# The first fold of the attention products: from a VectorE sum to an adding DMA of GpSimd

## The chip, the cores and the metric

The kernel runs on one core of a Trainium2 chip. The core has five engines with instruction queues of their own: TensorE (PE in the profile, with its weight loads as PEld), VectorE (DVE), ScalarE (ACT), GpSimd (POOL) and SyncE (SP). Data moves by 16 DMA engines; an engine's queue issues a transfer, and its end is told by a semaphore. The metric is the device time in microseconds (us) of one execution, taken as the median of several runs.

## What is computed

Two branches read the same layer-normalised input `xn` (2048 tokens, 512 features), and their outputs are added to `x`.

```
x  = A_x;  xn = layernorm(x)
q, k, v = split(xn @ wqkv)                 # 32 heads of 16
logits[s, w] = q[s] . k[s - 2 w] / 4       # w = 0..7, a dilated window of 8 keys
o[s] = sum_w softmax(logits)[s, w] v[s - 2 w]
A  = o @ wo
z  = gelu(xn @ w_in);  z1, z2 = halves of z (688 each);  z2 = layernorm(z2)
g  = w_sp @ z2 + b_sp                      # mixes over the 2048 tokens
B  = (z1 * g) @ w_out
out = x + A + B
```

The change lies in the logits of branch A.

## The kernel before, in words

The order of work on each of the five queues is written out by hand in five lists of names (`pe`, `act`, `dve`, `pool`, `sp`); a name stands for a few instructions, and `needs` says which names must be done first. A queue runs its list strictly in order: where one name waits, all names behind it on that queue wait as well.

TensorE goes through these stages: the z2 half of `w_in` (names z), the q and k heads (L350), the v heads (L350), the z1 half (names y, L247), the mixing over tokens (names M0 to M15, L512, 32 matmuls each), and the output products (L566, L573, L580). All of z, heads, y and M write to three PSUM buffers in turn: a stage step may start when ScalarE has emptied the buffer three steps back (M0 needs the emptying of y13, named yg13).

The attention logits are made without TensorE. q and k lie with 4 token groups of 32 heads on the 128 partitions. The 16 features of a head are dealt with in four chunks c = 0..3, and the tokens in two halves th = 0, 1, so there are eight units (c, th). A unit has three steps:

- `m{c}{th}` (products, L393): two VectorE multiplications of 128x4096 elements, one for each pair of features; where (c, th) is in `EARLY` the second is cut into two.
- `f{c}{th}` (fold, L398 or L401): the second 128x4096 array is added to the first. For seven units GpSimd issues two adding DMAs of 512 KB each (L401); for unit (0, 0) VectorE does one sum (L398).
- `p{c}{th}` (logits, L406 to L409): VectorE adds the two remaining features and the sum over chunks, in `a_sb`.

The units use four pairs of buffers. (0, 0), (1, 1) and (3, 0) share the first one, so m11 needs p00. The products of chunk c need k with its halo, the 16 keys that a token group takes from its neighbour. They are copied by small DMAs: `kh0a`, `kh0b` and `kh1` on SyncE's queue, `kh2` and `kh3` on GpSimd's (L368, L369). kh1 is made of 8 runs of 32 bytes per partition on 96 partitions and 4 on 32.

On VectorE stand between these steps the statistics of z2: zs8, zs12 (L307 to L310) and zb8, zb12 (L318), with zr8, zr12 (L314) on GpSimd between the two. After zb12 ScalarE normalises z2 tiles 12 to 15 (zn12 to zn15, L330), in turn with yg12 to yg15 (L339).

SyncE's queue at the time of the first units holds: kh0a, kh0b, W0, kh1, wv, W1, vh. W0 and W1 are transposing loads of 256 rows of `w_sp` (L489), wv loads the 512 KB of v weights (L258), vh copies v's halo. M0 needs W0, M2 needs W1.

GpSimd's queue at that time holds: zr4, kh2, f01, f10, zr8, f11, kh3, f20 and so on. kh2 waits for ScalarE's k casts of chunk 2 (L363).

Of the kernel before, what the change touches and what calls it, by code (L numbers as in the profile page):

```python
# [10 lines left out]
ALU = mybir.AluOpType  # L11
# [5 lines left out]
NT = S // P  # L17
# [25 lines left out]
def kernel(  # L43
# [13 lines left out]
    V = nc.vector  # L57
# [26 lines left out]
    b16 = sb.tile([NT, P], BF16, name="b16")  # L84
# [40 lines left out]
    ph = [[prod[n][:, a * PU // 2:(a + 1) * PU // 2] for a in range(2)] for n in range(2)]  # L125
# [268 lines left out]

    def fold(c, th):
        x = PU // 4
        if (c, th) == (0, 0):
            V.tensor_tensor(ph[0][0], ph[0][0], ph[0][1], ALU.add)  # L398
            return
        for n in range(2):  # L400
            G.dma_start(*[h[:, n * x:(n + 1) * x] for h in ph[BUF[c, th]]], accum_op=ALU.add)  # L401

# [8 lines left out]
    for c, th in BUF:  # L411
        n = f"{c}{th}"
        b = BUF[c, th]
        over = {2: ALLN + ALLX, 3: [f"p{1}{0}"] + [f"{a}{p}" for a in "qk" for p in range(8)]}.get(b, [])
        op_(f"m{n}", over + [f"qc{2 * c}", f"qc{2 * c + 1}"] + (["kh0a", "kh0b"] if c == 0 else [f"kh{c}"]) + ([last[b]] if b in last else []),
            lambda c=c, th=th: products(c, th))
        op_(f"f{n}", [f"m{n}"], lambda c=c, th=th: fold(c, th))
        op_(f"p{n}", [f"f{n}"], lambda c=c, th=th: logits(c, th))
        last[b] = f"p{n}"
# [249 lines left out]
    for i in range(6, NT):  # L669
        dve += [f"ag{i + 1}"] * (i + 1 < NT) + [f"b{i + 2}"] * (i + 2 < NT) + [f"n{i}"]  # L670
    dve += """zt0 zt1 zt2 zt3 zt4 zt5 zn0 zn1 zn2 zn3 zt6 zt7 zn4 zn5 zn6 zn7
        m00 f00 p00 m01 zs8 m10 m11 p01 zb8 m20 p10 m21 p11 zs12 m30 p20 zb12 m31 p21 p30 X0 HW p31 u0 X1 C0 g0 a0.0 u1 a0.1 C1 g1 g2
        a0.2 g3 a0.3 g4 a0.4 g5 a0.5 a0.6 g6 a0.7 g7 a0.8 a0.9 g8 a0.10 a0.11 g9 g10 a1.0 a1.1 g11 a1.2 g12 a1.3
        a1.4 g13 a1.5 g14 a1.6 a1.7 g15 a1.8 a1.9 a1.10 a1.11 a1.12 a1.13""".split()
    OUT = [i for n in range(3) for i in groups[n]] + tail
    dve += [f"F{i}" for i in OUT[:12]] + ["Fe"] + [f"F{i}" for i in OUT[12:]] + ["Fl0", "Fl1", "Fl2"]
    pool = ["b16"] + [f"gr{i}" for i in range(NT)] + "zr0 zr4 kh2 f01 f10 zr8 f11 kh3 f20 f21 zr12 f30 f31 LO5 V00 V01 V02 V03".split()
    sp = """x0 x1 x2 wz0 wz1 wz2 x3 x4 x6 wy x8 x12 wk t4 t5 t6 t7 t8 t9 t10 t11 t12 t13 t14 t15 wq kh0a kh0b W0 kh1 wv W1 vh
        W2 W3 LO0 LO1 W4 U0 W5 LO2 LO3 U1 U2 W6 LO4 U3 U4 W7 U5 U6 U7 U8 U9 U10 R0 U11 U12 U13 V10 V11 R1 U14 V12 U15 V13""".split()
    sp += [f"S{i}" for i in OUT] + ["Sl0", "Sl2"]  # L680
# [53 lines left out]
```

## Time and profile before

| | us |
|---|---|
| median of 3 runs | 200.03 (199.96 to 200.37) |
| profiled execution, whole time | 199.44 |
| its span, first to last instruction | 197.7 |
| TensorE busy | 192.8 (98% of the span) |
| VectorE busy | 179.2 (91%) |
| ScalarE busy | 87.9 (44%) |
| GpSimd busy | 43.4 (22%) |

The granted TensorE clock was 1.000. In the views shown below a row of a timeline gives the start in us, the duration in us, the engine, the line of the kernel, the operation, the output and input names, the shapes, the count of instructions merged into the row, and in brackets the idle time ahead of it with what ended it. A row of the DMA queues gives packets, megabytes, and the time that the packets took as a share of all 16 engines in that window: q0 holds what GpSimd issues, q1 what SyncE issues. This share can pass 100%, since a packet that is stalled counts for as long as it is open.

### The profile page before, as it was taken

How to read it: one execution, taken by the hardware profiler on the slowest of the kernel's cores; microseconds unless marked ns; L12 is line 12 of the kernel's file. 1: busy time of each engine (PE TensorE's matmuls, PEld its weight loads, DVE VectorE, ACT ScalarE, POOL GpSimd, SP SyncE). 2: the span in 40 equal slices, each digit the busy share in tenths (PEclk: the TensorE clock that was granted, in tenths of full speed). 3: DMA queues.
4: the chain of work that ended last, by engine and by line, in shares of the span. 5: the costliest groups of instructions: out<-in, count | busy, mean ns of one | idle time of the engine just before them, and what ended most of it. 6: DMA issues, size and time to landing. Idle time of an engine off the chain costs nothing.

```text
span 197.7 us, 4588 instructions
## 1 busy us (share of the span) xinstructions
PE 192.8 (98%) x1944; PEld 121.5 (61%) x1944; DVE 179.2 (91%) x214; ACT 87.9 (44%) x128; POOL 43.4 (22%) x79
## 2 busy tenths in 40 slices
PE   7899999999999999999999999999999999999993
PEld 2466666666666666666666666666666654444442
DVE  4899896799989999999999999999999999999073
ACT  2476798785558967792562311112221110044000
POOL 4477322001565326355000000011120000000000
PEclk9999999999999999999999999999999999999999
DMA  4999552499999999989699999999979227402433
GB/s 148 354 338 133 90 107 83 71 154 135 254 206 211 202 185 146 190 177 185 128 209 252 186 217 276 162 242 266 213 154 241 54 48 219 86 2 83 136 106 106
DMA packets 71252, 33.40 MB, mean 169 GB/s; under 512 B 59488, under 2 KB 69248, under 8 KB 71104
## 3 DMA queue, kind: packets, MB, share of 16 engines
q1 hardware_dynamic: 68400, 25.38, 61.6%
q0 software_dynamic: 2688, 7.70, 20.0%
q8 instruction: 15, 0.25, 0.5%
q10 hardware_dynamic: 144, 0.03, 0.1%
q14 instruction: 5, 0.04, 0.1%
HBM read 10.13 MB, written 2.10 MB: 62 GB/s over the span
## 4 chain that ended last, share of the span: by engine, by line
PE 93%; DMA 2%; SPq 1%; DVE 1%; issue 1%; DVEq 0%
PE mm L512 38%; PE mm L350 21%; PE mm L247 18%; PE mm L580 7%; PE mm L566 6%; PE aux L566 2%; DMA z<-in_A_x_dram 2%; PE mm L573 1%; SPq L255 1%; SPq L165 1%; PE aux L225 0%; DVE stats L172 0%; DVE z L628 0%; DVE z L186 0%; PE aux L580 0%
## 5 line engine op out<-in xcount | busy, mean ns | idle before, releaser
L512 PE MATMUL mm<-z,wsp 128*128 128x344 bf16 x512 | 74.8, 309 | 0.0
L512 PEld LDWEIGHTS <-wsp 128*128 128x128 bf16 x512 | 50.1, 98 | 24.6
L350 PE MATMUL mm<-xnT,wts 128*32 128x512 bf16 x768 | 41.7, 379 | 0.0
L247 PE MATMUL mm<-wts,xnT 128*128 128x344 bf16 x256 | 38.3, 309 | 0.0
L350 PEld LDWEIGHTS <-wts 128*32 128x32 bf16 x768 | 28.7, 139 | 12.8 <-issue 0.3
L460 DVE TENSOR_TENSOR prod<-vp,a_sb 128x4096 bf16<-128x4096 bf16 x16 | 36.2, 2282 | 0.0
L247 PEld LDWEIGHTS <-xnT 128*128 128x128 bf16 x256 | 24.6, 98 | 12.5 <-ACT xnT L228 0.6
L528 ACT ACTIVATE qk<-mm,b_col 128x688 bf16<-128x688 f32 x16 | 13.3, 830 | 42.4 <-PE mm L512 40.2
L393 DVE TENSOR_TENSOR prod<-qk 128x4096 bf16<-128x4096 bf16 (+1 forms) x15 | 27.2, 1860 | 1.2 <-ACT qk L363 1.1
L464 DVE TENSOR_TENSOR prod<-prod,prod 128x8192 bf16<-128x8192 bf16 (+1 forms) x7 | 26.7, 3809 | 0.1
L363 ACT CAST qk<-mm 128x1024 bf16<-128x1024 f32 x16 | 16.2, 1012 | 8.2 <-PE mm L350 8.2
L580 PE MATMUL mm<-wts,xnT 32*128 32x512 bf16 x192 | 14.5, 374 | 0.0
L523 POOL DMA_DIRECT2D qk<-qk x8 | 3.9, 497 | 47.9 <-DMA qk<-z 40.3
L339 ACT ACTIVATE z<-mm 128x688 bf16<-128x688 f32 x16 | 11.8, 742 | 4.2 <-PE mm L247 3.4
L264 ACT ACTIVATE z<-mm 128x688 bf16<-128x688 f32 x16 | 11.8, 744 | 3.2 <-PE mm L247 3.2
L566 PEld LDWEIGHTS <-qk 128*128 128x128 bf16 x75 | 7.3, 98 | 8.9 <-issue 0.4
L566 PE MATMUL mm<-wts,qk 128*128 128x512 bf16 x55 | 12.4, 379 | 0.0
L172 DVE BATCH_NORM_STATS2 stats<-z 128x6 f32<-128x512 bf16 x15 | 10.1, 673 | 2.0 <-DMA z<-in_A_x_dram 1.9
L401 POOL DMA_DIRECT2D prod<-prod x10 | 8.8, 978 | 11.6 <-DVE prod L393 11.6
L580 PEld LDWEIGHTS <-xnT 32*128 32x128 bf16 x256 | 6.7, 93 | 7.2
L183 POOL TENSOR_TENSOR rstd<-rstd,mhalf 128x1 f32<-128x1 f32 x16 | 9.0, 562 | 3.7 <-DVE rstd L200 2.6
L616 ACT CAST z<-mm 128x512 bf16<-128x512 f32 x6 | 3.3, 600 | 13.6 <-PE mm L580 13.6
(93 smaller groups left out, 179.0 us busy)
## 6 DMA issues: line engine op xcount, KB each, us to landing
prod<-prod POOLq DMA_DIRECT2D x10, 512.0 KB, 7.9
wts<-in_A_wo_dram SPq DMA_DIRECT2D x4, 512.0 KB, 6.7
wsp<-in_A_x_dram SPq DMA_DIRECT2D x2, 1024.0 KB, 6.5
out_dram<-z SPq DMA_DIRECT2D x15, 128.0 KB, 1.8
wts<-in_A_wqkv_dram SPq DMA_DIRECT2D x3, 512.0 KB, 6.4
z<-in_A_x_dram SPq DMA_DIRECT2D x2, 512.0 KB, 7.6
wsp<-z POOLq DMA_DIRECT2D x2, 512.0 KB, 8.8
wsp<-wts POOLq DMA_DIRECT2D x2, 512.0 KB, 8.4
```

Of the source, the lines that this page charges most:

```text
L247: PE.matmul(t[:, hh, 0:FHALF], xnT[:, kc, i * P:(i + 1) * P], w_z[part][:, kc, hh * FHALF:(hh + 1) * FHALF], start=(kc == 0), stop=(kc == ...
L264: A.activation(z2[:, i, :].rearrange("p (a b) -> p a b", a=2), t[:, :, 0:FHALF], ACT.Gelu_apprx_tanh, **total)
L339: op_(f"yg{i}", [f"y{i}"] + ["p10"] * (i >= 10), lambda: A.activation(z1u[:, i, 0:FH].rearrange("p (a b) -> p a b", a=2), t[:, :, 0:FHALF] ...
L350: PE.matmul(t[32 * g:32 * g + 32, dd, :], w, r, start=(kc == 0), stop=(kc == C - 1), tile_position=(0, 32 * g))
L363: op_(f"{a}c{p}", [f"{a}{p}"], lambda: A.copy(home(a, p), t[:].rearrange("p d (t s) -> p d t s", t=2)))
L393: V.tensor_tensor(pr[:, w0:w1], q[:, w0:w1], k[:, w0:w1], ALU.mult)
L460: return lambda: V.tensor_tensor(dst, vp[:, :, th, off:off + GS], a_sb[:, th, W - 1 - w].unsqueeze(1).broadcast_to([P, DH, GS]), ALU.mult)
L464: return lambda: V.tensor_tensor(dst, dst, x, ALU.add)
L512: PE.matmul(t[:, hh, 0:FHALF], w[:, k, (j % 2) * P:(j % 2 + 1) * P], z2[:, k, hh * FHALF:(hh + 1) * FHALF], start=(k == 0), stop=(k == NT ...
L528: lambda: A.activation(gs[j % 3].rearrange("p (a b) -> p a b", a=2), t[:, :, 0:FHALF], ACT.Identity, bias=b_col[:, j:j + 1]))
L566: PE.matmul(po[i][:, c], uT[th][:, m, t0:t0 + P], wout[:, m, c], start=(start and m == 0), stop=(stop and m == MF - 1))
L580: PE.matmul(po[groups[n][g]], op[32 * g:32 * g + 32, th, d, s * P:(s + 1) * P], wo_r[32 * g:32 * g + 32, d, :], start=False, stop=(d == DH ...
```

## The change

Unit (0, 0) loses its special case: its fold is done by two adding DMAs of 512 KB from GpSimd, as in the other seven units. On VectorE's list f00 leaves, and p00 (its logit sum) moves from ahead of m01 to behind m10, the products of the third unit. On GpSimd's list f00 stands ahead of kh2.

```
     def fold(c, th):
         x = PU // 4
-        if (c, th) == (0, 0):
-            V.tensor_tensor(ph[0][0], ph[0][0], ph[0][1], ALU.add)
-            return
         for n in range(2):
             G.dma_start(*[h[:, n * x:(n + 1) * x] for h in ph[BUF[c, th]]], accum_op=ALU.add)
...
-        m00 f00 p00 m01 zs8 m10 m11 p01 zb8 m20 p10 m21 p11 zs12 m30 p20 zb12 m31 ...
+        m00 m01 zs8 m10 p00 m11 p01 zb8 m20 p10 m21 p11 zs12 m30 p20 zb12 m31 ...
...
-    pool = [...] + "zr0 zr4 kh2 f01 f10 zr8 f11 kh3 f20 f21 zr12 f30 f31 LO5 V00 V01 V02 V03".split()
+    pool = [...] + "zr0 zr4 f00 kh2 f01 f10 zr8 f11 kh3 f20 f21 zr12 f30 f31 LO5 V00 V01 V02 V03".split()
```

More of the change, by code (lines that the diff above doesn't have):

```diff
@@ L671 @@
     dve += """zt0 zt1 zt2 zt3 zt4 zt5 zn0 zn1 zn2 zn3 zt6 zt7 zn4 zn5 zn6 zn7
-        m00 f00 p00 m01 zs8 m10 m11 p01 zb8 m20 p10 m21 p11 zs12 m30 p20 zb12 m31 p21 p30 X0 HW p31 u0 X1 C0 g0 a0.0 u1 a0.1 C1 g1 g2
+        m00 m01 zs8 m10 p00 m11 p01 zb8 m20 p10 m21 p11 zs12 m30 p20 zb12 m31 p21 p30 X0 HW p31 u0 X1 C0 g0 a0.0 u1 a0.1 C1 g1 g2
         a0.2 g3 a0.3 g4 a0.4 g5 a0.5 a0.6 g6 a0.7 g7 a0.8 a0.9 g8 a0.10 a0.11 g9 g10 a1.0 a1.1 g11 a1.2 g12 a1.3
@@ L676 @@
     dve += [f"F{i}" for i in OUT[:12]] + ["Fe"] + [f"F{i}" for i in OUT[12:]] + ["Fl0", "Fl1", "Fl2"]
-    pool = ["b16"] + [f"gr{i}" for i in range(NT)] + "zr0 zr4 kh2 f01 f10 zr8 f11 kh3 f20 f21 zr12 f30 f31 LO5 V00 V01 V02 V03".split()
+    pool = ["b16"] + [f"gr{i}" for i in range(NT)] + "zr0 zr4 f00 kh2 f01 f10 zr8 f11 kh3 f20 f21 zr12 f30 f31 LO5 V00 V01 V02 V03".split()
     sp = """x0 x1 x2 wz0 wz1 wz2 x3 x4 x6 wy x8 x12 wk t4 t5 t6 t7 t8 t9 t10 t11 t12 t13 t14 t15 wq kh0a kh0b W0 kh1 wv W1 vh
```

## The prediction

> **What bounds the kernel now.** I read the shares of busy time first, then the chain that ended last in order of time, then VectorE's, GpSimd's and SyncE's timelines around the change, then the DMA queues in small windows, and last the places where VectorE's work reaches TensorE.
>
> ```profile
> span 197.7 us, 4588 instructions
> PE 192.8 (98%) x1944; PEld 121.5 (61%) x1944; DVE 179.2 (91%) x214; ACT 87.9 (44%) x128; POOL 43.4 (22%) x79
> ...
> 10.27 19.54 PE mm L247 x134
> 29.81 41.60 PE mm L350 x768
> 71.41 15.27 PE mm L247 x104
> 86.68 74.67 PE mm L512 x512
> ```
>
> The chain's pieces follow each other without a hole: 10.27+19.54 = 29.81, +41.60 = 71.41, +15.27 = 86.68. From 10.27 us on TensorE streams and waits for nobody. So time taken off VectorE is worth nothing in itself. It can only make TensorE wait, if something comes later than it does now, or leave it alone. The question is whether a step of VectorE comes late, and how much slack it has.
>
> VectorE around the change:
>
> ```profile
> 36.24 4.50 DVE L393 TENSOR_TENSOR prod<-qk 128x4096 bf16<-128x4096 bf16 x2 [1.14 <-ACT qk L363]
> 40.78 2.29 DVE L398 TENSOR_TENSOR prod<-prod 128x4096 bf16<-128x4096 bf16 x1
> 43.10 1.22 DVE L406 TENSOR_TENSOR a_sb<-prod 128x2048 bf16<-128x2048 bf16 x1
> 44.24 4.56 DVE L393 TENSOR_TENSOR prod<-qk 128x4096 bf16<-128x4096 bf16 x3
> ...
> 49.58 2.29 DVE L393 TENSOR_TENSOR wsp<-qk 128x4096 bf16<-128x4096 bf16 x1
> ...
> 53.99 4.49 DVE L393 TENSOR_TENSOR prod<-qk 128x4096 bf16<-128x4096 bf16 x2
> 59.72 1.23 DVE L406 TENSOR_TENSOR a_sb<-prod 128x2048 bf16<-128x2048 bf16 x1 [1.25 <-DMA prod<-prod]
> ```
>
> These are m00, f00, p00, m01, m10 (from 49.58 to 53.99), m11 and p01. VectorE already waits once: p01 stands 1.25 us for the DMAs of f01 to land. Behind p01 it hardly rests: in the window 60 to 82 (TensorE, weight load, VectorE, ScalarE, GpSimd, each busy us and count) its 21.8 of 22 us are busy.
>
> ```profile
> 60.00:82.00 22.00, 22.00 (x286) 14.80 (x278) 21.78 (x19) 17.24 (x23) 10.21 (x10) 1.00 1.01 183
> ```
>
> So p01's start at 59.72 is what hands any delay on.
>
> **The change part by part.**
>
> Removed: f00 on VectorE, 40.78 to 43.10 = 2.32 us. p00 (43.10 to 44.24 = 1.14 us) is moved behind m10. Taken alone m10 would start 3.46 us earlier, at 46.1, and m11 would end 2.3 us earlier, at 56.1. p01 would then wait 3.6 us for f01 instead of 1.25, and start at 59.72 as now: worth 0.
>
> Added: two adding DMAs of f00. What they meet is seen on the two issuing queues, SyncE first:
>
> ```profile
> 35.84 6.18 SPq L489 DMA_TRANSPOSE wsp<-in_B_w_sp_dram  x1
> 42.12 0.62 SPq L368 DMA_DIRECT2D qk<-qk  x1
> 42.79 0.65 SPq L369 DMA_DIRECT2D qk<-qk  x1
> 43.49 0.59 SPq L258 DMA_DIRECT2D wts<-in_A_wqkv_dram  x1
> 44.13 7.36 SPq L489 DMA_TRANSPOSE wsp<-in_B_w_sp_dram  x1
> ```
>
> ```profile
> 48.60 0.86 POOL L368 DMA_DIRECT2D qk<-qk  x1 [15.10 <-ACT qk L363]
> 49.47 0.57 POOL L369 DMA_DIRECT2D qk<-qk  x1
> 50.03 1.86 POOL L401 DMA_DIRECT2D prod<-prod  x2
> ```
>
> GpSimd is idle for 15.10 us ahead of kh2, so issuing f00 (some 1.8 us by the row of f01) from 40.8 costs GpSimd nothing, and kh2 and f01 are issued when they are now. The cost is on the DMA engines. The rows of the queues in the windows 37 to 43.5, 43.5 to 44.6, 44.6 to 47.5, 47.5 to 49.5, 49.5 to 52.8, and (both rows of the last pair) 52.8 to 53.2:
>
> ```profile
> q1 hardware_dynamic: 4032, 1.03, 103.9%
> ...
> q1 hardware_dynamic: 1024, 0.05, 53.4%
> ...
> q1 hardware_dynamic: 807, 0.58, 79.5%
> ...
> q1 hardware_dynamic: 226, 0.07, 139.8%
> ...
> q1 hardware_dynamic: 3427, 0.88, 117.5%
> ...
> q0 software_dynamic: 80, 0.09, 107.0%
> q1 hardware_dynamic: 164, 0.04, 46.1%
> ```
>
> W0 fills the engines to 43.5. Then come kh1 (1024 small packets), wv, a stretch of 2 us in which W1 all but stands (226 packets), and W1 proper. kh2 and f01 were issued from 48.60 and 50.03 on, yet in 49.5 to 52.8 there isn't one packet of q0; q0 begins when W1 ends, at 52.9. From there f01 moves at q0's pace (first row below, the window 53.2 to 59.6):
>
> ```profile
> DMA packets 385, 1.33 MB, mean 207 GB/s; under 512 B 64, under 2 KB 64, under 8 KB 384
> ...
> q0 software_dynamic: 74, 0.30, 110.4%
> q1 hardware_dynamic: 90, 0.00, 7.1%
> ```
>
> A fold is 2 x 512 KB = 1.05 MB, which takes 1.05/0.207 = 5.1 us of all 16 engines. The last two rows are of 76 to 77.5, where a fold and v's halo (packets of 32 bytes) are both queued: 74 packets of the one went with 90 of the other, about one for one.
>
> With the change f00 is issued at 40.8, when m00 ends, and W0 still holds the engines to 43.5: f00 has 2.7 us to reach its queue unnoticed, and f01 needs at most 2.9 (50.03 to 52.9, W1 in its way). So it starts when W0 ends. Between 43.5 and W1's end the engines then have to do: kh1, 53.4% of 1.1 us = 0.6; f00, 5.1; wv, 79.5% of 2.9 us less a tenth for W1's first packets = 2.1; W1's 4096 packets at the pace of 3427 in 3.3 us = 3.9. Together 11.7 us, so W1 ends at 55.2 instead of 52.9. Put otherwise: of f00's 5.1 us some 2.8 fall into time that is now idle or stalled, and 2.3 push W1 back. f01, which cannot start before W1 is through, lands 2.3 later: p01 at 62.0 instead of 59.7. This is d = 2.3, with these ends: 0.3 if f01 gets its packets in ahead of W1 (then the next paragraph sets it), 4.3 if W1 again meets a stall of 2 us as it does now in 47.5 to 49.5. I take 2.3, the value by busy time, because both stalls now seen fall beside a wait for one late engine that the order of work may or may not repeat.
>
> kh1 comes late as well. It has some 60 packets on each engine against 16 of f00; one for one, it is done when f00 is, at 43.5+5.1+0.6 = 49.2. m10 then starts at 49.3, where it starts now at 49.58: what f00's removal gave is used up by this new wait. m10 takes 4.41, p00 1.14, m11 4.5: VectorE reaches p01 at 59.4 to 60.4, the later if one engine lags by 1 us. So even without f01 being late d is 0 to 0.7.
>
> What waits behind p01, and where d reaches TensorE:
>
> ```profile
> 82.20 0.16 DVE L318 TENSOR_TENSOR zbias<-zmean,zrstd 128x4 f32<-128x4 f32 x1
> ...
> 82.05 0.74 ACT L339 ACTIVATE z<-mm 128x688 bf16<-128x688 f32 x1 [0.42 <-PE mm L247]
> 82.69 0.95 ACT L330 ACTIVATE z<-z,zbias,zrstd 128x688 bf16<-128x688 bf16 x1
> ...
> 85.02 0.74 ACT L339 ACTIVATE z<-mm 128x688 bf16<-128x688 f32 x1
> ...
> 175.38 1.22 DVE L468 TENSOR_TENSOR xnT<-prod 128x2048 bf16<-128x2048 bf16 x1
> ...
> 178.31 3.46 PE mm L580 x64
> ```
>
> zb12 ends at 82.36, and ScalarE takes zn12 at 82.69 behind yg11: 0.33 of slack. From there ScalarE is packed, zn12, yg12, zn13, yg13; yg13 ends at 85.76, and M0, which needs its buffer, starts at 86.68: 0.92 more. So TensorE stands from d = 1.25 on, and by d - 1.25. Here d = 2.3 gives 1.05. Near the end the first attention half of the second output group (178.31) needs a sum that ends at 175.38+1.22 = 176.60: slack 1.7, which M0's stall has already made larger, so nothing is added there.
>
> The sum: 0 for f00 and p00, 0 on GpSimd, +1.05 by the late f01 at M0. The profiled execution took 199.44 at a span of 197.7, and 198.8 is forecast for such a span; the median of the runs shown is 200.03, 0.6 above that execution, and with 1.05 added gives 201.1.
>
> One rule of the Trainium skill speaks for another outcome. The page "DMA: Bandwidth & Descriptors", section "Queues, rings and completion order", says that each DMA engine takes its queues in turn, a packet at a time, of 64 descriptors at most. By that, kh2 and f01 should have had their turns inside W1; the row of 49.5 to 52.8 shows none in 3427 packets, some 214 per engine, so here a transposing load isn't broken up. Were the rule to hold with small packets, f01 would not be held by W1, and the time would be that of the second rival.
>
> **The rivals.**
>
> 1. A longer stall. W1 waits for the slowest engine, as in 47.5 to 49.5 now. If W1, moved to about 51 to 55, meets that again, 2.0 is added: d = 4.3, TensorE waits 3.05, 203.1. For it: the stall is there in the row of 226 packets. Against it: f00's own time may swallow it, as it lies where the stall is now.
> 2. No change. f01 gets its turn before or inside W1, because f00 delays wv so far that W1 isn't yet on the engines when f01 comes (50.03 and about 1 to 2 us), or because q0 is served in turn. Then f01 lands at 59 to 60, d is set by kh1 at 0 to 0.7, below 1.25: 200.0. It decides for this side as long as p01 starts before 60.97. For it: the slack of 1.25 is more than half of the 2.3. Against it: q0's silence in 49.5 to 52.8.
> 3. Faster. VectorE's saved 2.3 us would have to reach TensorE. No row shows TensorE waiting for VectorE after 10.27 us; only the last sums behind TensorE's end could move, and they don't depend on it. 199.5 at the best, if the profile hid such a wait.
>
> **How the numbers follow.** A difference of 0.2% (0.4 us) is about what a measurement of this kernel can tell from no change. Forecast, d between 1.65 and 3.3: 0.50. Rival 1: 0.15. Rival 2, with d up to 1.65: 0.30. Rival 3: 0.05. So slower 0.65, same 0.30, faster 0.05. The likeliest gives 201.1, with 200.4 to 202.1 as its own range (d of 1.65 to 3.3). The range for all reaches down to rival 2 (200.0, less 0.1 for the spread of runs) and up to d of 3.9, just short of rival 1's full 2 us: 199.9 to 202.7.
>
> **What would show each step.** Right: no L398 row, an idle stretch ahead of m10 that ends with kh1's landing at about 49; q0 packets from 43.5 on and none while W1 transposes; p01 starting at about 62 with a wait ended by the DMA; a wait of ScalarE ahead of zn12 (L330) for zb12, and a hole on TensorE between L247 and L512 of about 1 us; from there on the same pace. Wrong: m10 at 46.1 (kh1 not held back); p01 before 61.0 (then TensorE is untouched and the time stays); a hole on TensorE anywhere else, for instance at the v heads, if wv came later than they start.

## The result, and the profile after

The changed kernel takes 217.62 us (median of 6 runs) against 200.0 for the kernel before, also 6 runs. The ratio is 1.084, 95% interval 1.0789 to 1.089: 17.6 us slower, where 1.1 were forecast and 202.7 was the upper end of the range. Single executions of the changed kernel lie between 215.4 and 224.2, those of the kernel before between 199.8 and 200.4. The ratio is formed from the four faster executions of the changed kernel, 215.4 to 217.9; the two above 219 count as slow ones. The profiled execution took 216.67, its span is 214.9.

From the page of the changed kernel: the span, the busy times, two rows of the 40 slices (TensorE, and its granted clock), and two of the costliest groups with the idle time just before them in the last column.

```profile
span 214.9 us, 4589 instructions
PE 196.0 (91%) x1942; PEld 123.2 (57%) x1944; DVE 176.7 (82%) x213; ACT 88.0 (41%) x128; POOL 46.6 (22%) x81
...
PE   7899999999910399999999999999999999999993
...
PEclk9999999999975569999999999999999999999999
...
L350 PE MATMUL mm<-xnT,wts 128*32 128x512 bf16 x768 | 44.9, 397 | 13.4 <-issue 13.4
...
L403 DVE TENSOR_TENSOR a_sb<-prod 128x2048 bf16<-128x2048 bf16 x2 | 2.4, 1224 | 16.5 <-DMA prod<-prod 16.5
```

VectorE has lost its 2.3 us of work as meant (179.2 to 176.7). TensorE's busy time grew by 3.2 us, at the lower granted clock behind its hole, and GpSimd's by 3.2, of which 1.84 are the issuing of f00. There is one hole, from about 60 to 73 us, in which all the engines stand for most of the time. The two long idle times in it are TensorE's 13.4 us in the v heads (L350) and VectorE's 16.5 us ahead of a logit sum (L403, which was L406), which ended with the landing of an adding DMA.

VectorE's timeline around the change, with columns as in the rows of before; these are m10, p00, m11 and p01:

```profile
51.37 2.29 DVE L393 TENSOR_TENSOR wsp<-qk 128x4096 bf16<-128x4096 bf16 x1 [5.40 <-DMA qk<-qk]
...
55.78 1.22 DVE L403 TENSOR_TENSOR a_sb<-prod 128x2048 bf16<-128x2048 bf16 x1
57.03 4.49 DVE L393 TENSOR_TENSOR prod<-qk 128x4096 bf16<-128x4096 bf16 x2
77.98 1.23 DVE L403 TENSOR_TENSOR a_sb<-prod 128x2048 bf16<-128x2048 bf16 x1 [16.45 <-DMA prod<-prod]
```

m10 waits 5.40 us for kh1, so VectorE's saved time is gone, as forecast, and 2 us more with it (m10 was forecast for 49.3). Then p01 starts at 77.98 instead of 59.72, because f01 has not landed. Who issued what, on SyncE's queue (wv, W1) and on GpSimd's (f00, kh2, f01):

```profile
42.99 1.73 SPq L258 DMA_DIRECT2D wts<-in_A_wqkv_dram  x1
44.76 9.44 SPq L486 DMA_TRANSPOSE wsp<-in_B_w_sp_dram  x1
```

```profile
41.27 1.84 POOL L398 DMA_DIRECT2D prod<-prod  x2 [7.50 <-DVE prod L393]
48.81 0.86 POOL L368 DMA_DIRECT2D qk<-qk  x1 [5.70 <-ACT qk L363]
...
50.24 1.84 POOL L398 DMA_DIRECT2D prod<-prod  x2
```

kh2, f01 and W1 are issued within 0.7 us of the times they had before. What differs is on the DMA engines. The rows of the queues in the windows 54 to 56, 56 to 64 and 64 to 72.5 (packets, MB, share of 16 engines), and the rows of issues of the window 49 to 52 (last number: us from issue to landing):

```profile
q1 hardware_dynamic: 959, 0.25, 104.5%
q0 software_dynamic: 58, 0.09, 66.6%
...
q0 software_dynamic: 161, 0.57, 65.5%
q1 hardware_dynamic: 337, 0.09, 52.3%
...
q0 software_dynamic: 292, 1.03, 85.8%
q1 hardware_dynamic: 327, 0.08, 18.0%
q8 instruction: 1, 0.02, 5.6%
...
prod<-prod POOLq DMA_DIRECT2D x2, 512.0 KB, 26.1
qk<-qk POOLq DMA_DIRECT2D x1, 24.0 KB, 24.5
wsp<-in_B_w_sp_dram SPq DMA_TRANSPOSE x1, 30.2
```

Before, W1 landed 12.4 us after its issue, f01 8.1 and kh2 5.3; now it is 30.2, 26.1 and 24.5. W1 has most of its packets through by 56. From 54 on q0's packets move beside W1's, and from 55 on both move at a fraction of their pace: from 56 to 72.5 q1 gets 664 packets through in 16.5 us, where the kernel before had 3427 through in 3.3. A packet of q1 takes 52.3% x 16 engines x 8 us / 337 = 0.20 us in the window 56 to 64, and one of q0 65.5% x 16 x 8 / 161 = 0.52 us. In the rows of the kernel before W1's packets took 117.5% x 16 x 3.3 / 3427 = 0.018 us, with nothing of q0 beside them. This is called the crawl below.

How it reaches the end. TensorE's timeline, first of the kernel before (start of the heads; M0), then of the changed kernel, and one row of ScalarE's timeline, zn12:

```profile
29.74 41.67 PE L350 MATMUL mm<-xnT,wts 128*32 128x512 bf16 x768
...
86.52 74.83 PE L512 MATMUL mm<-z,wsp 128*128 128x344 bf16 x512
```

```profile
29.95 30.22 PE L350 MATMUL mm<-xnT,wts 128*32 128x512 bf16 x553
73.53 14.72 PE L350 MATMUL mm<-xnT,wts 128*32 128x512 bf16 x215 [13.37 <-issue]
...
103.76 74.83 PE L509 MATMUL mm<-z,wsp 128*128 128x344 bf16 x512 [0.16 <-ACT z L339]
```

```profile
100.64 0.96 ACT L330 ACTIVATE z<-z,zbias,zrstd 128x688 bf16<-128x688 bf16 x1 [0.99 <-DVE zbias L318]
```

The heads start 0.21 us later in this execution, so p01 is 77.98 - 0.21 - 59.72 = 18.05 late, and M0 103.76 - 0.21 - 86.52 = 17.03. The span is 17.2 longer. M0 waits for ScalarE, and ScalarE waits at zn12 for VectorE's zb12: the chain that the prediction described, with another size of d.

TensorE's own hole in the v heads has another cause. Its releaser is "issue": it waited for nothing that the profile shows, and what it lacked was probably instructions. The q8 row above is one packet of the instruction queue (0.02 MB), and 5.6% of 16 engines over 8.5 us make 7.6 us for it. In the kernel before that queue has one packet in 53.2 to 59.6 and one in 61 to 63, and the second takes 3.0% x 16 x 2 = 0.96 us (row below). In the changed kernel the windows from 49 to 64 show none, so the fetch came late as well as slowly. The trace doesn't name whose instructions a packet holds; but TensorE stops behind the 553rd matmul of the heads here, and behind the same one in two later runs that crawl.

```profile
q8 instruction: 1, 0.02, 3.0%
```

When TensorE went on, its granted clock was 0.56 (window 75 to 80; the last numbers are clock, DMA share and GB/s):

```profile
75.00:80.00 5.00, 5.00 (x59) 2.79 (x52) 2.00 (x3) 1.70 (x2) 0.34 (x1) 0.56 0.60 116
```

Two explanations of the 17 us were therefore open: the late fold, which holds VectorE, and the missing instructions with the lowered clock, which hold TensorE.

### The profile page after: what moved, and what is told of

Read it like the earlier page. It is cut to its first block, busy times and chain, and to the rows that moved or that the text cites. A ratio compares the mean times of both kernels' runs of the same rounds, so it can differ in the third digit from the quotient of the medians.

```text
span 214.9 us, 4589 instructions
## 1 busy us (share of the span) xinstructions
PE 196.0 (91%) x1942; PEld 123.2 (57%) x1944; DVE 176.7 (82%) x213; ACT 88.0 (41%) x128; POOL 46.6 (22%) x81
## 4 chain that ended last, share of the span: by engine, by line
PE 64%; DMA 18%; DVE 9%; issue 4%; ACT 2%; SPq 1%; POOL 0%; DVEq 0%; ACTq 0%
PE mm L509 35%; DMA prod<-prod 12%; PE mm L247 10%; PE mm L577 6%; PE mm L563 5%; DMA qk<-qk 4%; PE mm L350 4%; DVE prod L393 3%; PE aux L563 2%; DMA z<-in_A_x_dram 2%; DVE a_sb L406 1%; DVE prod L405 1%; DVE z L393 1%; DVE wts L393 1%; ACT qk L363 1%
## 5 line engine op out<-in xcount | busy, mean ns | idle before, releaser
L350 PE MATMUL mm<-xnT,wts 128*32 128x512 bf16 x768 | 44.9, 397 | 13.4 <-issue 13.4
L350 PEld LDWEIGHTS <-wts 128*32 128x32 bf16 x768 | 30.4, 141 | 27.7 <-issue 16.8
L247 PE MATMUL mm<-wts,xnT 128*128 128x344 bf16 x256 | 38.4, 309 | 0.0
L247 PEld LDWEIGHTS <-xnT 128*128 128x128 bf16 x256 | 24.5, 98 | 12.6 <-ACT xnT L228 0.7
L363 ACT CAST qk<-mm 128x1024 bf16<-128x1024 f32 x16 | 16.2, 1012 | 8.2 <-PE mm L350 8.2
L403 DVE TENSOR_TENSOR a_sb<-prod 128x2048 bf16<-128x2048 bf16 x2 | 2.4, 1224 | 16.5 <-DMA prod<-prod 16.5
L398 POOL DMA_DIRECT2D prod<-prod x12 | 10.7, 974 | 23.9 <-DVE prod L393 23.9
L363 ACT CAST vp<-mm 128x1024 bf16<-128x1024 f32 x8 | 8.0, 1006 | 17.3 <-PE mm L350 17.2
```

The costliest lines, as they stand in the source:

```text
L247: PE.matmul(t[:, hh, 0:FHALF], xnT[:, kc, i * P:(i + 1) * P], w_z[part][:, kc, hh * FHALF:(hh + 1) * FHALF], start=(kc == 0), stop=(kc == ...
L350: PE.matmul(t[32 * g:32 * g + 32, dd, :], w, r, start=(kc == 0), stop=(kc == C - 1), tile_position=(0, 32 * g))
L363: op_(f"{a}c{p}", [f"{a}{p}"], lambda: A.copy(home(a, p), t[:].rearrange("p d (t s) -> p d t s", t=2)))
```

## The experiments

Theory A: W1, pushed back by f00, meets GpSimd's adding DMAs, both crawl, and the late fold delays TensorE by d - 1.25. Rivals: the order of VectorE's work costs the time; f00's traffic alone does; the hole on TensorE is the instruction fetch; any large load beside a fold would crawl, not only a transposing one. Beside each run the kernel before was measured on the same chip (medians of 199.66 to 200.09). No kernel came out faster than it.

### The order alone

The kernel before, with only p00 moved:

```
-  m00 f00 p00 m01 zs8 m10 m11 p01 ...
+  m00 f00 m01 zs8 m10 p00 m11 p01 ...
```

> The kernel before, with only p00 moved behind m10; its fold stays a sum on VectorE. If the new order of VectorE costs the time, this is slower by much of the 17 us. If the two added DMAs do it (collision or longer queue), VectorE does the same work in another order, p01 still starts when f01 lands (59.7), and the time is that of before within 0.4 us.

199.7 against 199.81, ratio 0.9991 [0.9975, 1.0007]. The order is not the cause.

### The change without W1

```
-  SP.dma_start_transpose(wsp[n % 3], ...)
+  if n != 1: SP.dma_start_transpose(wsp[n % 3], ...)      # M2, M3 read W0's rows
```

> The changed kernel without the load W1 (M2 and M3 read W0's rows of w_sp instead, so the output of those 256 tokens is another one); all folds as in the changed kernel. Collision theory: f01 lands at 58 to 60, no hole on TensorE, d below 1.25: 200.0 within 0.5 us. Theory that the added traffic or the late halo copy costs the time whatever else is in flight: above 205.

200.47 against 199.81, ratio 1.0056 [1.003, 1.0083]. VectorE's m10 and p01:

```profile
51.62 2.30 DVE L393 TENSOR_TENSOR wsp<-qk 128x4096 bf16<-128x4096 bf16 x1 [5.43 <-DMA qk<-qk]
...
61.70 1.22 DVE L403 TENSOR_TENSOR a_sb<-prod 128x2048 bf16<-128x2048 bf16 x1
```

f00 and kh1 are as in the changed kernel, but there is no hole, and p01 does not wait for f01. It comes 1.56 us later than before all the same, which was expected to stay below 1.25. So without W1 f00 costs 0.7 us by the medians (0.6 to 1.7 by the interval; the ten executions lie between 200.2 and 202.3), through the late kh1; W1 has to be there for the other 17.

### The folds held until W1 has landed

```
+  op_("HOLD", ["W1"], G.tensor_scalar(dep, wsp_r[1][0:1, 0:2], ...))   # reads what W1 writes
-  pool = ... zr4 f00 kh2 f01 ...
+  pool = ... zr4 f00 HOLD kh2 f01 ...
```

> The changed kernel, with one read of W1's first bytes by GpSimd ahead of kh2, so that kh2 and f01 are issued only when W1 has landed. f00's DMAs stay as they are. Collision theory (W1 and the folds slow each other to a crawl when they are on the DMA engines together): W1 ends at about 55.5, f01 is issued at about 57.5 and lands at about 65, no crawl; d = 5 at p01, and by the slack of 1.25 TensorE waits 3 to 5 us: 203 to 205. Theory that f00's traffic itself or the late halo copy costs the time: it stays near 217.

208.32 against 199.81, ratio 1.0428 [1.0386, 1.047]: half of the loss is gone, but not as much as expected (203 to 205). The held read and f01 on GpSimd, and p01:

```profile
58.18 1.72 POOL L486 TENSOR_SCALAR dep<-wsp 1x2 f32<-1x2 bf16 x1 [14.88 <-DMA wsp<-in_B_w_sp_dram]
...
61.30 1.87 POOL L398 DMA_DIRECT2D prod<-prod  x2
```

```profile
68.66 1.23 DVE L403 TENSOR_TENSOR a_sb<-prod 128x2048 bf16<-128x2048 bf16 x1 [6.61 <-DMA prod<-prod]
```

With the folds kept off it, W1 lands at 58 instead of about 75 (its packets are through at about 56), and f01 lands some 7 us after its issue. No crawl; what is left is the hold itself, which put f01's issue to 61.3, where 57.5 was expected.

### W1 put into the folds, without f00's DMAs

The kernel before, W1 waiting for a small write of GpSimd behind f01:

```
+  op_("HX", [], G.memset(wsp_r[1][0:1, 0:2], 0.0))        # W1 overwrites it
-  pool = ... kh2 f01 f10 ...
+  pool = ... kh2 f01 HX f10 ...
```

> The kernel before, with its fold on VectorE, but W1 held back by a GpSimd write into its buffer behind f01's issue, so that it is issued at about 52, into the folds. No f00 DMA at all. Collision theory: W1 crawls beside the folds and f01 lands late, as in the changed kernel: 208 or more, with a hole on TensorE in the v heads if the instruction fetch is caught as well. Theory that the added 5.1 us of fold traffic is the cause: W1 isn't needed before M2, so the time is that of before within 1 us.

219.36 against 199.81, ratio 1.0981 [1.0943, 1.1018]. From the rows of issues in the window 50 to 56, and VectorE's p10, which waits for f10:

```profile
wsp<-z POOLq DMA_DIRECT2D x2, 512.0 KB, 29.8
...
wsp<-in_B_w_sp_dram SPq DMA_TRANSPOSE x1, 31.4
```

```profile
86.43 1.23 DVE L408 TENSOR_TENSOR wsp<-wsp 128x2048 bf16<-128x2048 bf16 x1 [19.34 <-DMA wsp<-z]
```

The crawl is there in full with VectorE still doing f00: W1 takes 31.4 us and f10 29.8. It was f10 that was caught, and not f01 as expected: p01 starts at 61.28. The crawl needs W1 and a fold at the same time, not the change as such.

### W1 ahead of f00

The changed kernel with another order on SyncE's queue, all work kept:

```
-  sp = ... wq kh0a kh0b W0 kh1 wv W1 vh
+  sp = ... wq W0 kh0a kh0b W1 kh1 wv vh
```

> The changed kernel with W0 issued ahead of kh0a and W1 ahead of kh1, so that both transposing loads are through at about 44, when f00 starts; all work is kept. Collision theory: no crawl, 200 to 201.5 (kh1 and VectorE still late by f00's traffic). If f00's traffic costs the time without W1 beside f01: above 205. If f00 meets the end of W1 at 43: a crawl there, above 205 too, with kh1 landing after 55.

200.18 against 200.09, ratio 1.0011 [0.9995, 1.0027]. W1's issue, and VectorE's m10 and p01:

```profile
38.01 5.46 SPq L486 DMA_TRANSPOSE wsp<-in_B_w_sp_dram  x1
```

```profile
49.37 2.29 DVE L393 TENSOR_TENSOR wsp<-qk 128x4096 bf16<-128x4096 bf16 x1 [1.41 <-DMA qk<-qk]
...
59.78 1.23 DVE L403 TENSOR_TENSOR a_sb<-prod 128x2048 bf16<-128x2048 bf16 x1 [0.25 <-DMA prod<-prod]
```

The same eight folds by DMA cost nothing when W1 is through before f01 starts. They gain nothing either.

### Half of the fold

The changed kernel with one of f00's two DMAs; VectorE sums the other half (`fh`) behind m00:

```
+  G.dma_start(first halves, accum_op=ALU.add);  fh: V.tensor_tensor(second halves, ALU.add)
-  m00 m01 zs8 m10 p00 ...
+  m00 fh m01 zs8 m10 p00 ...
```

> The changed kernel with only the first 512 KB of f00 as an adding DMA; VectorE sums the other half (1.2 us) behind m00. If the collision has a threshold, W1 moves back by about half as much, ends at about 54, and f01, queued from 51 on, waits for it as before the change or is caught in it: either about 200 or about 215, hardly between. If the loss goes with the bytes of f00, half of the 17 us: 208 to 209.

199.88 against 200.09, ratio 0.9992 [0.9978, 1.0007]. p01 starts at 60.05 after 2.95 us of waiting. Half the traffic does not cost half of the loss but none of it. The rows say why: W1's last packets pass at about 53, as in the kernel before, so f01 does not meet it.

### The late fold by itself

The kernel before with small instructions of GpSimd ahead of f01, so that the fold is late with no collision: 26 of them, and 4.

```
+  op_("DLY", [], [G.tensor_tensor(dly, rstd[:, 0:1], mhalf[:, 0:1], ALU.pow) for _ in range(26)])   # or 4
-  pool = ... kh2 f01 ...
+  pool = ... kh2 DLY f01 ...
```

> The kernel before, with 26 small GpSimd operations ahead of f01, so that f01 is issued some 15 to 20 us late, long after W1 has ended. Nothing collides. If the late folds alone explain the changed kernel, the time rises by the delay of p01 less 1.25 us: 213 to 219, with ScalarE waiting for zb8 and TensorE for ScalarE in the v heads. If the hole on TensorE by the stuck instruction fetch is a cost of its own, this stays well below the changed kernel for the same delay of p01.

> The kernel before, with 4 small GpSimd operations ahead of f01: f01 is issued 2 to 5 us late, and nothing collides. By the slack of 1.25 the time rises by the delay of p01 less 1.25 us, 0.8 to 3.8; if the slack is larger than read (2.5 or more), by half of that or nothing.

220.19 against 200.09, ratio 1.1013 [1.099, 1.1035], with 26; 206.94, ratio 1.0346 [1.0326, 1.0366], with 4. Both are more than expected (219 and 203.9 at the most), because the instructions delayed p01 more than was reckoned, by 20.27 and 6.65 us. With 26, p01, TensorE's hole, and zn8 on ScalarE:

```profile
80.22 1.23 DVE L406 TENSOR_TENSOR a_sb<-prod 128x2048 bf16<-128x2048 bf16 x1 [21.52 <-DMA prod<-prod]
```

```profile
83.46 6.84 PE L350 MATMUL mm<-xnT,wts 128*32 128x512 bf16 x96 [17.01 <-ACT vp L363]
```

```profile
81.55 0.96 ACT L330 ACTIVATE z<-z,zbias,zrstd 128x688 bf16<-128x688 bf16 x1 [19.21 <-DVE zbias L318]
```

A fold that is merely late costs what the changed kernel loses, without a crawl. TensorE stops in the v heads here too, now because ScalarE has not emptied its buffers: ScalarE's queue stands at zn8, which needs zb8, and zb8 stands behind p01 on VectorE. So in the changed kernel TensorE would probably have stopped in the v heads even with its instructions there. With 4, a second, small hole stands near the end, ahead of the second attention half:

```profile
185.96 3.63 PE L583 MATMUL mm<-wts,xnT 32*128 32x512 bf16 x64 [0.96 <-DVE xnT L468]
```

Now the runs in which p01 is late can be held against the prediction's step "TensorE waits d - 1.25". In the table d is p01's start less 59.72 and M0's lateness its start less 86.52, each less the difference in the start of the heads to 29.74; the span's growth is to 197.7, less the same difference.

| kernel | d | d - 1.25 | M0 later | span longer |
|---|---|---|---|---|
| W1 as an ordinary load (below) | 1.52 | 0.27 | 0.50 | 0.43 |
| without W1 | 1.56 | 0.31 | 0.54 | 0.58 |
| W1 in pieces of 256 bytes (below) | 3.28 | 2.03 | 2.27 | 2.25 |
| 4 small instructions | 6.65 | 5.40 | 5.74 | 6.84 |
| folds held for W1 | 8.53 | 7.28 | 7.76 | 8.19 |
| the changed kernel | 18.05 | 16.80 | 17.03 | 16.99 |
| 26 small instructions | 20.27 | 19.02 | 19.26 | 20.57 |

M0 is late by d - 1.25 plus 0.2 to 0.5 everywhere, from 1.5 us to 20. Where d is below 1.25 (p00 moved, half of the fold, W1 ahead of f00), M0 isn't late at all. From p01's start to M0's it is 26.80 us in the kernel before, and 25.78 to 25.80 in the changed kernel, with 26 small instructions, without W1, in both runs with an ordinary load and in the four runs of the last experiment. Some of these have a hole on TensorE and some have none. So the slack as measured is 1.02 us, and in the changed kernel the stuck fetch and the lowered clock added nothing to the loss: TensorE ran again at 73.5, and M0 could not have started earlier than it did. With the folds held it is 26.03 us; there nothing stands ahead of M0 but TensorE's own work, which had run at a granted clock of 0.50 behind its hole (72 to 76). In three runs the span grew by 0.4 to 1.3 more than M0 was late, and there the second hole (0.32, 0.96 and 1.17) stands near the end.

### W1 as an ordinary load

The changed kernel, W1 loaded by an ordinary DMA of the same bytes; first with 8 KB to a partition, then in runs of 256 bytes, as many pieces as the transposing load has.

```
-  SP.dma_start_transpose(wsp[1], B_w_sp[2 * P:4 * P, :])
+  SP.dma_start(wsp_r[1], B_w_sp[2 * P:4 * P, :].rearrange("(p b) s -> p (b s)", p=P))
   # or "(b p) (k q) -> p k b q", q=128
```

> The changed kernel in which W1 is loaded by an ordinary DMA of the same 1.05 MB, 8 KB to a partition, instead of the transposing one (block 1 of the weights is then not transposed, so the numbers that the mixing multiplies by are other ones; no work is left out). Theory (the transposing form of the load is what crawls beside the adding DMAs): no crawl. W1 and f01 may share the engines, but their times add: from about 51 the engines have W1 (at most 5 us at 207 GB/s) and f01 (5.1 us) to do, so f01 lands by 61 at the latest and p01 starts between 60 and 62; 200 to 201.5 against 200.0. Rival (any 1.05 MB load that is still running when GpSimd's DMAs are issued makes both crawl): f01 lands 20 us or more after its issue, p01 at 70 or later, a hole of over 5 us on TensorE, 208 or more.

> As the run before, with W1 by an ordinary DMA in runs of 256 bytes, so that it has 4096 pieces as the transposing load has (the block again isn't transposed, and no work is left out). Theory (the transposing form is the cause): no crawl, W1 and f01 in turn; W1's 256 pieces per engine against f01's 16 and kh2's 24 let f01 through first, p01 at 60 to 62, 200 to 201.5. Rival (small packets beside large ones are the cause, in turns of one for one): W1 lands 20 us or more after its issue and f01 late with it, p01 at 66 or later, 205 or more.

200.29 against 200.06, ratio 1.0015 [1.0002, 1.0028], and 201.77, ratio 1.0077 [1.0052, 1.0101]. The second was expected at 201.5 at the most. With 8 KB, W1's issue row and p01:

```profile
wsp<-in_B_w_sp_dram SPq DMA_DIRECT2D x1, 1024.0 KB, 11.0
```

```profile
61.91 1.22 DVE L403 TENSOR_TENSOR a_sb<-prod 128x2048 bf16<-128x2048 bf16 x1
```

In pieces of 256 bytes: W1's issue row, the queues in the window 64 to 70, p01, and TensorE's wait:

```profile
wsp<-in_B_w_sp_dram SPq DMA_DIRECT2D x1, 1024.0 KB, 28.1
...
q0 software_dynamic: 322, 1.18, 99.0%
q1 hardware_dynamic: 240, 0.06, 7.4%
```

```profile
63.05 1.23 DVE L403 TENSOR_TENSOR a_sb<-prod 128x2048 bf16<-128x2048 bf16 x1 [1.64 <-DMA prod<-prod]
```

```profile
87.36 1.33 PE L247 MATMUL mm<-wts,xnT 128*128 128x344 bf16 x8 [1.48 <-ACT z L339]
```

Neither crawls. In the first W1 is all but through when f01's packets come (32 packets of q1 are left at 53.5), so it is the second that tests the overlap: there some 970 of W1's pieces are left when f01's first packets of 4 KB move, at 54.95, about as many as in the changed kernel (1030, below). In the second W1 is slow as well, 28.1 us, which half of the rival had said. But the folds aren't: q0 moves 1.18 MB in 6 us with 99.0% of the engines, 0.295 us a packet (99.0% x 16 x 6 / 322), and a packet of W1 costs 0.030. Where a transposing load has 0.20 and makes q0's packet take 0.52, an ordinary one of small pieces only takes its turns in between. So it is the transposing form that makes both queues slow. Whether it takes adding DMAs on the other side, or any with packets of 4 KB, was not tried.

### Who comes first?

Left open was why folds already issued waited for W1's end in the kernel before, and broke into it in the changed one. In the kernel before W1's packets flow from about 49.5 on and f01 is issued at 50.03. In the changed kernel W1 starts at about 51.5, behind f00, kh1 and wv, and f01 (50.24) has been issued by then. The theory: whoever is there first keeps the engines. Four runs put small instructions of GpSimd into the changed kernel, to move kh2 or f01 behind W1's first packets.

```
-  pool = ... f00 kh2 f01 ...
+  pool = ... f00 DLY kh2 f01 ...          # DLY: one small instruction
+  pool = ... f00 kh2 DLY f01 ...          # one; then two of them
+  pool = ... f00 DEP DLY kh2 f01 ...      # DEP: a read of k's third chunk, which waits for the casts
```

> The changed kernel with one small instruction of GpSimd (a power of 128 elements, about 2.2 us, its result used by nobody) ahead of kh2, waiting for the same k casts as kh2, so that kh2 is issued at about 51.0 and f01 at about 52.5, when W1's first packets are already moving (51 to 51.5). All work is kept. Theory (who comes first decides: adding DMAs that find the transposing load already moving wait for its end, as in the kernel before; those that lie queued when it starts break into it): no crawl, W1 ends at about 55.5, f01 lands at about 61, p01 at 61 to 62.5; 200.2 to 201.7 against 200.0, a gain of some 16 us on the changed kernel by an added instruction. Rival (f00's traffic leaves the 16 engines out of step, and whoever is queued breaks in on the engines that are through, whenever it was issued): the crawl as in the changed kernel, p01 at 72 or later, 210 or more.

> As the run before, but the small instruction stands between kh2 and f01: kh2 is issued at 48.8 as in the changed kernel, ahead of W1's first packets, f01 at about 52.5, behind them. Theory (who comes first decides): kh2's 28 KB lie ahead of W1 and may break in, but f01 doesn't; if the crawl needs f01's large transfer to be queued first, p01 comes at 61 to 63 and the time is 200.2 to 202; if kh2's few packets are enough to start it, it is 208 or more. Rival (engines out of step): the crawl as in the changed kernel in both runs, 210 or more.

> The changed kernel with two of the small instructions between kh2 and f01, so that f01 is issued at about 54.9, over 3 us behind the first packets of W1 (51 to 51.5). All work is kept. Theory (adding DMAs that find the transposing load already moving wait for it, those that lie queued when it starts break into it): no crawl in any execution; W1 ends at about 56, f01 lands at 62 to 63, p01 at 62 to 65, d of 2.5 to 5; 201 to 204 with executions that agree within 1 us, where the run with one instruction spread over 203.6 to 216.3. Rival (f00's traffic leaves the engines out of step, and that alone lets queued folds break in): executions of 210 and more, or a spread of over 5 us, again.

> The changed kernel with a read of two elements of k's third chunk by GpSimd (which waits for the same casts as kh2) and one small instruction ahead of kh2, so that kh2 is issued at 51 to 51.5 and f01 at 52.5 to 53, both behind W1's first packets. All work is kept. Theory (who comes first decides): no crawl, or in fewer executions than with kh2 at 48.97 and f01 at 52.64; p01 at 61 to 65, 200.5 to 204. Rival (engines out of step): the crawl as in the changed kernel in at least half of the executions, 210 or more.

The first edit moved nothing. The instruction did not wait for the casts, whose data it doesn't read, and ran at 42.29, kh2 and f01 were issued at 48.62 and 50.07 as in the changed kernel, and the time was 219.34: a repeat of the changed kernel, with p01 at 79.47. The others, with f01's issue, the packets of W1 (of 4096) that are left when f01's first packet of 4 KB moves, and W1's time from issue to landing, all in the profiled execution (203.6 in the third row):

| | f01 issued | W1 left | W1 to landing | p01 | executions |
|---|---|---|---|---|---|
| changed kernel | 50.24 | 1030 | 30.2 | 77.98 | 215.4 to 224.2 |
| read and one ahead of kh2 | 51.17 | 570 | 24.1 | 73.31 | 211.3 to 215.6 |
| one ahead of f01 | 52.64 | 70 | 16.7 | 64.87 | 203.6, 203.9, 213.8, 216.3 |
| two ahead of f01 | 52.18 | 140 | 16.2 | 65.49 | 203.9 to 207.2 |

The small instructions were shorter than expected (0.6 us each in the second and the last row's run), so f01 never came as late as 54.9. With two ahead of f01 (205.66 against 199.66 by the medians) neither expectation held: the executions reach up to 207.2, above the theory's 204, and differ by 3.3 us, but none comes to the rival's 210. With the read ahead of kh2 (212.75 against 199.66) all four executions came out as the rival had it, above 210. With two ahead of f01, p01:

```profile
65.49 1.23 DVE L403 TENSOR_TENSOR a_sb<-prod 128x2048 bf16<-128x2048 bf16 x1 [3.13 <-DMA prod<-prod]
```

Two microseconds later with f01 take 12 us off the time. But who comes first does not decide by itself. In the changed kernel, too, W1's packets first pass at full pace with none of q0 among them, 2 to 4 us after f01's issue. And kh2's small packets, which came in alone with one instruction ahead of f01, did not start a crawl. The rows of the changed kernel in 52 to 54, then of that run in 54 to 56:

```profile
q1 hardware_dynamic: 1995, 0.51, 114.9%
...
q1 hardware_dynamic: 1520, 0.39, 131.0%
q0 software_dynamic: 64, 0.03, 5.9%
```

f01's first packet of 4 KB moves 3.0 us after its issue in the kernel before (at 53.0, when W1 is just through), and 4.6 us after it in the changed kernel (at 54.8). It was held off longer there, and beside the ordinary load of 256-byte pieces too (4.9 us), so the wait is nothing peculiar to a transposing load. What differs is how much of W1 is left when these packets come, and the table follows that: next to nothing (6 packets) in the kernel before, 1030 packets in the changed one. What holds q0 off for 3 to 5 us, and lets it in then, is not shown, and why one kernel gave both outcomes at 52.64 isn't either: only the one of 203.6 was profiled.

## Why the prediction missed

The sign was right and the size wrong: 201.1 was forecast, with 1.05 us of loss, and 17.6 came. By its steps:

- **VectorE's 2.3 us are worth nothing.** Right. TensorE did not wait for VectorE, and in the runs without a crawl the saved time became a wait at p01 (2.95 us in the run with half the fold) or at m10.
- **The order of p00 costs nothing.** Right: 0.9991 [0.9975, 1.0007].
- **kh1 comes late, one for one with f00.** Right in kind; m10 starts at 51.37, forecast 49.3. VectorE was to reach p01 by 59.4 to 60.4 and got there at 61.53 (77.98 - 16.45). The term that was too small is f00's 5.1 us: its packets run from about 43 until after 49. In the run without W1 this alone makes d = 1.56 and costs 0.7 us: rival 2 with a d a little larger than its 0.7.
- **W1 is pushed back.** Right: it starts about 2 us later, and with the folds held off it, its packets are through at about 56, forecast 55.2.
- **"f01, which cannot start before W1 is through, lands 2.3 later".** This is the step that failed. It rested on the row of 49.5 to 52.8 of the kernel before, with 3427 packets of W1 and none of q0, read as "a transposing load isn't broken up". That row showed only that f01 had to wait for 3.0 us, at the end of which W1 was through. In the changed kernel f01 waited for 4.6 us and then moved beside the last 1030 packets of W1: q0 has 58 packets in 54 to 56 beside 959 of q1, and then both crawl. f01 landed about 18 us later than before, not 2.3. The forecast and its first two rivals, the longer stall too, took it for granted that two transfers that share the engines add up their times.
- **TensorE waits d - 1.25, by way of zb12, zn12 and M0.** Right in its path, and within 0.5 us for d from 1.5 to 20; the slack is 1.02 us by the runs, where 1.25 was read. The run in which W1 is an ordinary load of 256-byte pieces shows the forecast chain as a whole, though not for the forecast reason: d = 3.28, a hole of 1.48 us in L247 ahead of M0, 201.77.
- **Nothing is added near the end.** Right for the changed kernel (span 16.99 longer, M0 17.03 later); wrong by 0.3 to 1.2 us in three of the runs.
- **A hole elsewhere would be a sign of an error.** It was: TensorE stood at the v heads. The prediction had followed p01 to zb12 alone; for a large d zb8, directly behind p01, stops ScalarE's v casts earlier. In the changed kernel it was the late instructions that stopped TensorE first.

The rule of the Trainium skill that was weighed, from the page "DMA: Bandwidth & Descriptors", section "Queues, rings and completion order", that a DMA engine takes its queues in turn, fits the changed kernel (q0 and q1 side by side from 54 on) and the run with pieces of 256 bytes (322 and 240 packets in 6 us). It does not fit the silent 3.3 us of the kernel before, nor 52 to 54 in the changed one. From it the prediction had concluded that f01 would then not be held by W1 and the time stay at 200.0; by the rows it is the reverse, since a turn beside a transposing packet costs 0.2 us instead of 0.018.

## What to carry to other kernels

Before a transfer is added to a busy stretch, list what else will be in flight there, and treat a transposing load beside GpSimd's adding DMAs as a collision of its own kind, whose price isn't the sum of the two times: keep one wholly ahead of the other, as the run with W1 moved ahead did. A row that shows two queues not mixing tells only that one of them waited for that long in that run; it is no proof that it waits for the other's end. When the outcome turns on such a meeting, the range has to hold the case that both get slow, and the chain behind it (here d - 1.25) should be worked out for large delays as well as for small ones.

## What the runs showed of the hardware that was not expected

- A transposing load (256-byte packets) and adding DMAs (4 KB) on the same engines: 0.20 and 0.52 us a packet, against 0.018 for the first alone and 0.295 for the second beside an ordinary load of 256-byte pieces. Together 82 GB/s in 56 to 64 (0.57 + 0.09 MB in 8 us), where the fold of the kernel before had 207.
- One or two microseconds decide how much of it there is: with f01 issued at 50.24, 51.17 and 52.18, some 1030, 570 and 140 packets of W1 were left when f01's came, and W1 took 30.2, 24.1 and 16.2 us to land.
- In the kernel before, a single packet of the instruction queue stands just ahead of each stall of a transposing load: one in 40.0 to 40.5, and q1 has 22 packets in 41 to 42; one in 47.0 to 47.5, and q1 has 24 in 48.0 to 49.5. The second is the stall of 2 us that the prediction put down to a late engine. That the packet causes the stall is not tested.
- The instruction queue uses the same DMA engines: in the crawl one packet of it came late and took 7.6 us instead of 0.96, and TensorE stood 13.4 us with "issue" as the releaser, with a granted clock of 0.56 afterwards. Here it was hidden behind the late fold; a kernel in which nothing else waits would probably have paid for it.
